# Seven-product passes: a second buffer for the first product's copy, and a hand-laid order on every engine from step 28 on

## The chip, the cores and the metric

The kernel runs on one core of a Trainium2 chip. A core has a matrix engine (PE, TensorE), three engines that work on vectors (DVE, VectorE; ACT, ScalarE; POOL, GpSimd), and queues that move data between HBM and the on-chip memory SBUF; the kernel starts its transfers from SP (SyncE). PE writes into eight accumulator banks of 128x512 numbers. The metric is the device time of one execution, in microseconds (us), smaller is better. The kernel before took 745.49, 742.14 and 744.34 us in three runs, median 744.34.

## The reference

Three stages, each on the result of the one before, all in float32:

```
# 1: attention in chunks of 32 tokens (4 x 8 heads x 768 tokens x 64), with 8 memory keys
a = softmax(0.125 * q_c @ k_full.T);  x = a @ v_full           # x: 3072 x 512
# 2: a feed-forward layer, 512 -> 2048 -> 512
r = maximum(x @ w_in, 0);  y = (s * (r * r) + b) @ w_out        # s, b: one number each
# 3: a soft mixture of 8 experts with 4 slots each
logits = y @ phi                                                # 3072 x 32
slots  = softmax(logits over tokens).T @ y
out    = softmax(logits over slots) @ (maximum(slots @ w1, 0) @ w2)
```

## The kernel before

**Tiles.** The 3072 tokens are six blocks of 512. Every product of stage 2 is worked out from two fp32r pieces: an operand is split into a "high" piece (ACT rounds it) and a "low" piece (DVE or POOL takes the difference), and high x high, high x low and low x high are summed in a bank: three matmuls for one. A split therefore costs an ACT instruction and then a DVE or POOL instruction, and PE waits for the second one.

**Blocks 0 and 1** are worked out in 32 plain steps n. Step n is `mm_h(n)` (12 matmuls, L320, into bank 4 or 5 in turn), `make_g` (L326 to L329: relu on ACT, times on DVE, high on ACT, low on DVE), a few background tasks, and `mm_y(n-1)` (12 matmuls, L339). The background tasks are pieces of attention units u = 0 to 23 (four to a block): `qk` (L192, followed by exp and norm on DVE and ACT), `tr` (a transpose, L221, that ACT L224 and DVE L228 copy out of the bank) and `pv` (L235, copied out by ACT L241, for blocks 2 to 5 as raw x). From step NF-4 on, `pv` uses the bank of L320 that the next step's `mm_h` will use.

**Blocks 2 to 5** are worked out in two calls of `super_block(s)`, each for two blocks and in eight passes p. A pass does a 2x2 block product with seven products instead of eight (`prod`, L623, six matmuls, some 1.36 us each): a11, s1, s2, then 12 matmuls of the second layer (L339) for the pass before, s4, s3, 12 more, a22, a12. All seven go through four banks A, B, C, D. The product a11 stays in bank A: its copy c11 is taken out of it by ACT L687, then s2 is added onto it in the same bank. At the end of the pass, a12 is added to c11 (DVE L722), c11 is squared through a relu (ACT L637, DVE L638) and split into the tile G[0] (ACT L633, DVE L634). c21, from a22, gets the same chain into G[1]. c11 and c21 are the two halves of the tile y0.

`w_sums` (POOL L596) makes the sums of the weights that a pass needs, `w_split` (ACT L615, POOL L616) splits them, `wo_split` (ACT L628, POOL L629) those of the second layer; `wi_load` and `wo_load` bring the weights. In the passes of s = 0 the pieces of units 17 to 23 stand between the products. In the first passes also stand the tasks of the third stage for an older block (`log`, `etr`, `ytr`, `slot`): `log` runs a chain of small DVE instructions and three ACT instructions (L372, L377, L379). After its passes `super_block` has 16 `t2` jobs of 12 matmuls, with the x sums and splits for the next call beside them, or with the loads of the experts' weights.

**Order.** PE and SP run in the order of the program text. ACT, DVE and POOL run in an order that the framework's scheduler chose from its own cost model, except in the opening and the last stage. On every engine the instructions start strictly one after the other: an instruction that waits holds up all behind it.

Of the kernel before, what the change touches and what calls it, by code (L numbers as in the profile page):

```python
# [38 lines left out]
def tile_attention_moe_softmoe(  # L39
# [532 lines left out]
    def wi_load(p):  # L572
        sp.dma_start(out=fresh(f"sp{4 + p}") if p < 2 else cur[f"sp{4 + p % 2}"], in_=DWI[p])
# [57 lines left out]
    def g_split(t, dst):  # L631
        g = hl(dst)
        act.activation(out=r32(g[:, 0]), in_=t, func=AF.Identity, bias=b_col)  # L633
        dve.scalar_tensor_tensor(out=r32(g[:, 1]), in0=t, scalar=b_col, in1=g[:, 0], op0=ALU.add, op1=ALU.subtract)  # L634

    def square(out, h, r):
        act.activation(out=r, in_=h, func=AF.Relu, scale=1.0 / WSCALE ** 2)  # L637
        dve.scalar_tensor_tensor(out=out, in0=h, scalar=s_col, in1=r, op0=ALU.mult, op1=ALU.mult)  # L638

    def super_block(s, pending):  # L640
# [10 lines left out]
        def spot(p, k):  # L651
            if (p, k) in routing:
# [3 lines left out]
            if s == 0:  # L656
                u = 4 * NHP + p
                if k == 1 and p < NPR - 1:
                    run_bg("qk", u + 1, D)
                elif k == 2:  # L660
                    run_bg("pv", u, B)
                elif k == 3 and p < NPR - 1:
                    run_bg("tr", u + 1, D)

        gring = ["sp4", "sp5", "g1", "g0"] * 2 + ["sp5", "g1", "g0"] * 3
        wring = ["sp6", "wi1", "wo1", "wo0"] * 2 + ["rt1", "wo1", "wo0"] * 3
# [15 lines left out]
        fresh("rt1")  # L682
        for p in range(NPR):
            if p + 1 < NPR:
                wi_load(p + 1)
# [6 lines left out]
            if p + 1 < NPR:
                w_sums(p + 1)
                w_split(0, p + 1)
                w_split(1, p + 1)
            else:
                prep(0)
# [7 lines left out]
            square(cur[G2[p]], CH[1], cur["rt1"])  # L705
            if p + 1 < NPR:
# [18 lines left out]
            if p + 1 < NPR:  # L725
                w_split(3, p + 1)
            spot(p, 3)
            pending.append(lambda p=p: mm_job(yp, WO[1], G[1], p == 0, False))
            pending.append(lambda p=p: mm_job(yp, WO[0], G[0], False, p == NPR - 1))
            if s and p == 0:  # L730
                for t in [cur[f"x0{h}"] for h in range(NHP)] + Q + K + V + PB + [EP]:
                    e_free(t)

# [6 lines left out]
        if s == 0:  # L740
# [17 lines left out]
            task(12, w_split, 3, 0)  # L758
        else:
# [6 lines left out]
            for i, t in ((5, "sp4"), (5, "sp6"), (6, "wi1"), (10, "w10"), (10, "w11"), (10, "w12"), (10, "w13"),  # L766
                         (14, "g0"), (14, "wo0"), (15, "sp5"), (15, "wo1"), (15, "g1")):
# [23 lines left out]
    with tc.manual_schedule(engines={mybir.EngineType.PE, mybir.EngineType.SP}):  # L791
# [61 lines left out]
        for n in range(NSTEP):  # L853
# [4 lines left out]
            if n == NSTEP - 1:  # L858
                w_sums(0)
                w_split(0, 0)  # L860
            mm_h(n, (3,) if n == 0 else (0, 1, 2, 3))
# [16 lines left out]
            if n in (NF + 3, NF + 7, NF + 11):  # L878
                for kt in range(2):
                    if n == NF + 11:  # L880
                        x_sum("t1", 0, kt)
                    x_split({3: "b11", 7: "b21", 11: "t1"}[n - NF], 0, kt)
            if n in (NF + 13, NF + 15):
                kt = (n - NF - 13) // 2
                x_sum("t2", 0, kt)
                x_split("t2", 0, kt)
                x_split("b22", 0, kt)
                x_sum("t3", 0, kt)
                x_split("t3", 0, kt)
# [6 lines left out]
            if n == NSTEP - 1:
                w_split(1, 0)
                w_split(2, 0)
                w_split(3, 0)
# [257 lines left out]
```

## Time and profile before

| | |
|---|---|
| runs | 745.49, 742.14, 744.34 us, median 744.34 |
| profiled execution | 743.28 us |
| its span, first to last instruction | 741.5 us |
| busy in the span | PE 678.4, DVE 412.2, ACT 387.0, POOL 289.5 us |
| plain steps 28 to 31 | about 210 to 242 us |
| passes of s = 0, its t2 jobs | about 242 to 417, 417 to 478 us |
| passes of s = 1, its t2 jobs | about 478 to 631, 631 to 685 us |

Busy PE time is made of matmuls at the clock that the chip grants to TensorE: PEclk 1.00 is the upper of its two levels, 0.50 the lower. A stretch is therefore worth two readings, the part of it in which PE stands idle, and the clock in the rest.

### The profile page before, as it was taken

What the parts mean: (1) busy time and instruction counts of PE and PEld (TensorE: products, weight loads), DVE (VectorE), ACT (ScalarE), POOL (GpSimd) and SP (SyncE); (2) the same over time, 40 slices, a digit from 0 to 9 for tenths busy, and PEclk for the clock granted to TensorE, in tenths of its full rate; (3) what the DMA queues carried; (4) which work ended last, traced back from release to release, by engine and by line L of the source; (5) the groups of instructions that cost most, each with busy time, mean ns of one, the idle gap of its engine ahead of it and who ended that gap; (6) DMA issues with size and microseconds to landing.
All of it is one profiled execution on the core that took longest, in us unless ns stands there. A gap on an engine that the chain in (4) does not pass through costs nothing.

```text
span 741.5 us, 12554 instructions
## 1 busy us (share of the span) xinstructions
PE 678.4 (91%) x4983; PEld 528.2 (71%) x4983; DVE 412.2 (56%) x692; ACT 387.0 (52%) x688; POOL 289.5 (39%) x261
## 2 busy tenths in 40 slices
PE   7899999999999788898888799986998888999996
PEld 4678888888788567777766487864776666787474
DVE  4899986665567566544555646445333333532423
ACT  4898864655455455444445555444444544643322
POOL 4100001333458645445555647437355653422000
PEclk9999999999999899999999899999999999999998
DMA  9999945632435132333210230083101110998796
GB/s 333 408 378 371 340 143 197 188 128 92 138 119 194 57 139 93 139 121 108 86 57 28 78 122 29 29 333 149 57 21 40 72 44 23 359 400 301 284 375 270
DMA packets 37786, 126.90 MB, mean 171 GB/s; under 512 B 4192, under 2 KB 4192, under 8 KB 37728
## 3 DMA queue, kind: packets, MB, share of 16 engines
q1 hardware_dynamic: 37728, 126.11, 45.8%
q8 instruction: 39, 0.64, 0.4%
q14 instruction: 19, 0.16, 0.1%
HBM read 111.41 MB, written 14.68 MB: 170 GB/s over the span
## 4 chain that ended last, share of the span: by engine, by line
PE 69%; DVE 8%; DMA 8%; ACT 6%; POOL 6%; issue 2%; SPq 1%; DVEq 0%; POOLq 0%; ACTq 0%
PE bank L339 33%; PE bank L623 12%; PE bank L320 9%; DVE g L634 3%; PE bank L192 3%; PE bank L235 2%; PE bank L1019 2%; ACT g L633 2%; PE bank L978 2%; PE bank L387 2%; DMA sp4n<-dwi 2%; DMA sp<-wd 1%; DVE y L638 1%; POOL sp6n L596 1%; DMA q<-e1d 1%
## 5 line engine op out<-in xcount | busy, mean ns | idle before, releaser
L339 PE MATMUL bank<-g,wo 128*128 128x512 f32 x984 | 247.9, 403 | 0.0
L339 PEld LDWEIGHTS bank<-g,wo 128*128 128x128 f32 x984 | 185.4, 193 | 43.5 <-issue 2.5
L320 PE MATMUL bank<-x,wi 128*128 128x512 f32 x384 | 93.1, 391 | 0.2 <-DVE x L251 0.2
L629 POOL TENSOR_TENSOR wo<-yt,wo 128x512 fp32r<-128x512 f32 x36 | 48.8, 1355 | 92.5 <-ACT wo L628 92.5
L320 PEld LDWEIGHTS bank<-x,wi 128*128 128x128 f32 x384 | 71.8, 188 | 15.5 <-DVE x L251 0.6
L304 POOL TENSOR_TENSOR wi<-w,wi 128x512 fp32r<-128x512 f32 x16 | 20.5, 1281 | 112.6 <-ACT wi L300 111.3
L628 ACT ACTIVATE wo<-yt 128x512 fp32r<-128x512 f32 x36 | 22.7, 630 | 44.1 <-PE bank L339 43.8
L623 PE MATMUL bank<-w6n,wi1n 128*128 128x512 f32 x48 | 16.9, 464 | 31.4 <-ACT y L687 31.2
L702 DVE TENSOR_TENSOR y<-bank,y 128x512 f32<-128x512 f32 x16 | 11.1, 692 | 58.5 <-PE bank L623 58.3
L634 DVE SCALAR_TENSOR_TENSOR g<-y,cons,g 128x512 fp32r<-128x512 f32 x32 | 34.9, 1089 | 12.4 <-ACT g L633 11.5
L327 DVE SCALAR_TENSOR_TENSOR rt<-bank,cons,rt 128x512 f32<-128x512 f32 x32 | 23.9, 746 | 28.7 <-ACT rt L326 28.5
L313 POOL TENSOR_TENSOR wo<-w,wo 128x512 fp32r<-128x512 f32 x16 | 21.1, 1318 | 44.4 <-ACT wo L312 44.4
L623 PEld LDWEIGHTS bank<-w6n,wi1n 128*128 128x128 f32 x48 | 8.7, 205 | 38.3 <-ACT y L687 37.3
L300 ACT ACTIVATE wi<-w 128x512 fp32r<-128x512 f32 x32 | 20.1, 627 | 29.4 <-PE bank L320 29.4
L312 ACT ACTIVATE wo<-w 128x512 fp32r<-128x512 f32 x32 | 20.1, 628 | 23.8 <-PE bank L339 23.0
L192 PEld LDWEIGHTS bank<-k,q 128*64 128x64 f32 x704 | 24.7, 150 | 8.1 <-issue 5.7
L633 ACT ACTIVATE g<-y,cons 128x512 fp32r<-128x512 f32 x32 | 22.9, 715 | 11.4 <-DVE y L638 11.4
L235 PEld LDWEIGHTS bank<-pb,v 128*64 128x64 f32 x704 | 22.4, 138 | 8.9 <-issue 3.8
L192 PE MATMUL bank<-k,q 128*64 128x64 f32 x704 | 27.7, 237 | 1.1 <-ACT ep L208 1.1
L638 DVE SCALAR_TENSOR_TENSOR y<-bank,cons,rt 128x512 f32<-128x512 f32 x16 | 12.0, 750 | 30.1 <-ACT rt L637 29.4
L329 DVE SCALAR_TENSOR_TENSOR g<-rt,cons,g 128x512 fp32r<-128x512 f32 x32 | 25.9, 809 | 3.1 <-ACT g L328 2.6
L616 POOL TENSOR_TENSOR w14n<-sp6n,w14n 128x512 fp32r<-128x512 f32 x16 | 21.3, 1328 | 14.6 <-ACT w14n L615 14.6
(489 smaller groups left out, 1546.2 us busy)
## 6 DMA issues: line engine op xcount, KB each, us to landing
sp<-wd SPq DMA_DIRECT2D x24, 512.0 KB, 9.8
k<-kd SPq DMA_DIRECT2D x22, 512.0 KB, 5.2
v<-vd SPq DMA_DIRECT2D x22, 512.0 KB, 3.6
q<-qd SPq DMA_DIRECT2D x20, 512.0 KB, 3.9
yt<-dwo SPq DMA_DIRECT2D x18, 512.0 KB, 3.3
dwi<-w SPq DMA_DIRECT2D x16, 256.0 KB, 7.2
dwo<-w SPq DMA_DIRECT2D x16, 256.0 KB, 7.2
sp4n<-dwi SPq DMA_DIRECT2D x8, 512.0 KB, 4.2
```

What stands on the lines that cost most here:

```text
L192: pe.matmul(S[64 * par:64 * par + 64, 2 * i + z, :], lhsT=qt[:, c].rearrange("p h n -> p (h n)"), rhs=kt[:, c, :], start=True, stop=True)
L235: pe.matmul(b[64 * h:64 * h + 64, 64 * m:64 * m + 64], lhsT=vt[:, m, h, :], rhs=pb[:, m // 2, m % 2, h].rearrange("p z n -> p (z n)"), sta ...
L320: pe.matmul(HB[n % 2], lhsT=r32(w[:, a, kt, :]), rhs=r32(x[:, b]), start=(kt == 0 and i == 0), stop=(kt == 3 and i == 2))
L327: dve.scalar_tensor_tensor(out=t, in0=HB[n % 2], scalar=s_col, in1=r, op0=ALU.mult, op1=ALU.mult)
L329: dve.scalar_tensor_tensor(out=r32(g[:, 1]), in0=t, scalar=b_col, in1=g[:, 0], op0=ALU.add, op1=ALU.subtract)
L339: pe.matmul(yb[dt], lhsT=r32(w[:, a, dt * 128:dt * 128 + 128]), rhs=r32(g[:, b]), start=(first and i == 0), stop=(last and i == 2))
L616: pool.tensor_tensor(out=r32(lo), in0=src, in1=hi, op=ALU.subtract)
L623: pe.matmul(b, lhsT=r32(wv[:, a, kt, :]), rhs=r32(xv[:, c]), start=(first and kt == 0 and i == 0), stop=(kt == 1 and i == 2), skip_group_c ...
L628: act.activation(out=r32(t[:, 0]), in_=src, func=AF.Copy)
L629: pool.tensor_tensor(out=r32(t[:, 1]), in0=src, in1=t[:, 0], op=ALU.subtract)
L633: act.activation(out=r32(g[:, 0]), in_=t, func=AF.Identity, bias=b_col)
L634: dve.scalar_tensor_tensor(out=r32(g[:, 1]), in0=t, scalar=b_col, in1=g[:, 0], op0=ALU.add, op1=ALU.subtract)
```

## The change

- The copy of a11 goes to the two halves of y0 in turn (`p % 2`). c21 loses its half there and stays, with its relu and square, in one half of the tile rt0; the square of c11 goes into the other half (t11).
- The split of t11 into G[0] moves from the end of a pass behind the c11 copy of the next pass (`finish`). The two copies of a transpose move behind that as well; the transposes themselves stay at the end of the pass.
- `w_sums` and the weight splits of a pass are spread over it in another order; `wi_load(p + 2)` is issued inside pass p, where `wi_load(p + 1)` stood at its head.
- Units 8 to 16 of the attention, and the x splits, come one plain step earlier. The `pv` of unit 15 now stands in step 29 and uses bank 4, that of unit 16 in step 31, bank 4 too, which is bank A of the first pass. `w_sums(0)` moves to step 30.
- From step 28 to the last t2 job ACT, DVE and POOL run in the order of the program text.

```diff
     for u in range(2 * NHP, 4 * NHP + 1):
-        n0 = NF - 3 + 2 * (u - 2 * NHP)
+        n0 = NF - 4 + 2 * (u - 2 * NHP)
...
-        c11, c21 = hl(CH[0])[:, 0], hl(CH[0])[:, 1]
-        r11, r21 = hl(RT[0])[:, 0], hl(RT[0])[:, 1]
+        t21, t11 = hl(RT[0])[:, 0], hl(RT[0])[:, 1]
...
+        def finish(p):
+            g_high(t11, G[0])
+            g_low(t11, G[0])
+
         for p in range(NPR):
-            if p + 1 < NPR:
-                wi_load(p + 1)
+            c11 = hl(CH[0])[:, p % 2]
+            more = p + 1 < NPR
             prod(A, "a11", "b11", p)
             act.activation(out=c11, in_=A, func=AF.Copy)
+            if p:
+                finish(p - 1)
+                if s == 0:
+                    att_place(4 * NHP + p, D)
+            if more:
+                w_sums(p + 1)
+            w_split(3, p)
+            wi_load(p + 2)
             prod(C, "s1", "t1", p)
             act.activation(out=c22, in_=C, func=AF.Copy)
+            if more:
+                w_split(0, p + 1)
+            else:
+                prep(0)
             prod(A, "s2", "t2", p, False)
...
-            square(c21, A, r21)
-            g_split(c21, G[1])
+            prod(A, "a22", "t4", p, False)
+            relu(t21, A)
+            times(t21, A, t21)
+            prod(B, "a12", "b21", p)
             dve.tensor_tensor(out=c11, in0=B, in1=c11, op=ALU.add)
-            square(c11, c11, r11)
-            g_split(c11, G[0])
-            if p + 1 < NPR:
-                w_split(3, p + 1)
-            spot(p, 3)
+            g_high(t21, G[1])
+            relu(t11, c11)
+            g_low(t21, G[1])
+            times(t11, c11, t11)
+            if s == 0 and more:
+                att_turn(4 * NHP + p + 1, D)
...
-            if n in (NF + 13, NF + 15):
-                kt = (n - NF - 13) // 2
+            if n in (NF + 12, NF + 14):
+                kt = (n - NF - 12) // 2
                 x_sum("t2", 0, kt)
-                x_split("t2", 0, kt)
-                x_split("b22", 0, kt)
                 x_sum("t3", 0, kt)
-                x_split("t3", 0, kt)
+                for op in ("b22", "t2", "t3"):
+                    x_split(op, 0, kt)
                 x_sum("t4", 0, kt)
                 x_split("t4", 0, kt)
...
+            if n == NSTEP - 2:
+                w_sums(0)
...
+        for n in range(NSTEP - 4):
+            plain_step(n)
+        with tc.manual_schedule(engines={mybir.EngineType.Activation, mybir.EngineType.DVE, mybir.EngineType.Pool}):
+            for n in range(NSTEP - 4, NSTEP):
+                plain_step(n)
+            super_block(0, [last_plain, lambda: None])
+            super_block(1, [lambda: y_evac(yb=bank[4:8]), lambda: None])
```

On ACT at the turn from one pass of s = 1 to the next, before. y0 holds c11 and c21, rt0 the relus, bank 0 is bank A; L637 is a relu, L633 a high piece, L687 the copy of a11:

```order
L637 ACTIVATE rt0_97<-bank0_159 128x512
L615 ACTIVATE w15n_3976<-sp4n_3882 128x512
L633 ACTIVATE g1_96<-y0_109,cons_66 128x512
L637 ACTIVATE rt0_97<-y0_109 128x512
L633 ACTIVATE sp4n_4801<-x10n_2385,cons_66 128x512
L633 ACTIVATE g0_95<-y0_109,cons_66 128x512
L689 ACTIVATE y1_110<-bank2_161 128x512
L615 ACTIVATE wi0n_3929<-sp5n_4026 128x256
L687 ACTIVATE y0_109<-bank0_159 128x512
```

The same place now (L650 is the relu, L643 the high piece, L702 the copy of a11):

```order
L635 ACTIVATE wo0_85<-yt1_108 128x512
L650 ACTIVATE rt0_97<-bank0_159 128x512
L643 ACTIVATE g1_96<-rt0_97,cons_66 128x512
L650 ACTIVATE rt0_97<-y0_109 128x512
L702 ACTIVATE y0_109<-bank0_159 128x512
L643 ACTIVATE g0_95<-rt0_97,cons_66 128x512
L622 ACTIVATE w15n_4038<-sp4n_3884 128x512
L712 ACTIVATE y1_110<-bank2_161 128x512
```

The copy of a11 stood behind the high piece of g0 and two more; it now stands ahead of it, directly behind the relu of c11.

On ACT in steps 28 to 30, before. bank 5 and bank 4 are those of `mm_h`, L326 the relu and L328 the high piece of `make_g`, L241 the copy of a `pv`, L563 a high piece of an x split:

```order
L208 ACTIVATE ep_111<-ep_111 128x512
L615 ACTIVATE w14n_2379<-sp6n_2319 128x512
L326 ACTIVATE rt0_97<-bank4_163 128x512
L615 ACTIVATE wi0n_2324<-sp4n_2183 128x256
L241 ACTIVATE x03n_1382<-bank5_164 128x512
L328 ACTIVATE g0_95<-rt0_97,cons_66 128x512
L563 ACTIVATE w9n_2365<-x03n_1382 128x512
```

The same copy (unit 15, now L247) and what stands ahead of it now; L569 is the x split's high piece, L306 and L318 the high pieces of `split_wi` and `split_wo`, L332 and L334 the relu and the high piece of step 29:

```order
L208 ACTIVATE ep_111<-ep_111 128x512
L569 ACTIVATE w8n_2220<-x02n_1328 128x512
L569 ACTIVATE w6n_2223<-x00n_1326 128x512
L569 ACTIVATE w10n_2226<-x00n_1326 128x512
L569 ACTIVATE w12n_2230<-x00n_1326 128x512
L306 ACTIVATE wi0_83<-w14_81 128x512
L318 ACTIVATE wo1_86<-w13_80 128x512
L332 ACTIVATE rt1_98<-bank5_164 128x512
L334 ACTIVATE g1_96<-rt1_98,cons_66 128x512
L247 ACTIVATE x03n_1329<-bank4_163 128x512
```

The copy now stands behind four x splits and behind the whole of step 29's chain on ACT, and it reads bank 4, which `mm_h(30)` takes next. On ACT at the head of the first pass, as it is now (L622 is a weight split, L247 the copy of unit 16's `pv`):

```order
L318 ACTIVATE wo1_86<-w15_82 128x512
L622 ACTIVATE wi0n_2349<-sp4n_2233 128x256
L622 ACTIVATE w14n_2352<-sp6n_2342 128x512
L332 ACTIVATE rt1_98<-bank5_164 128x512
L334 ACTIVATE g1_96<-rt1_98,cons_66 128x512
L622 ACTIVATE wi1n_2371<-sp6n_2342 128x512
L247 ACTIVATE x00n_1326<-bank4_163 128x512
L702 ACTIVATE y0_109<-bank4_163 128x512
```

The copy of unit 16 used to stand in the first pass, out of bank B; it now reads bank 4, the bank of the first product, behind two weight splits that wait for `w_sums(0)`.

## Rows read from the trace of the kernel before

**Rows 1.** The page: busy us, share of the span and instructions of each engine.
```profile
PE 678.4 (91%) x4983; PEld 528.2 (71%) x4983; DVE 412.2 (56%) x692; ACT 387.0 (52%) x688; POOL 289.5 (39%) x261
```

**Rows 2.** Waits: engine, line, waited for; us in total, times, longest.
```profile
PE bank L623 <- ACT y L687: 31.2, 13, 3.5
```

**Rows 3.** Stretches: us, busy PE, PEld, DVE, ACT, POOL, clock, DMA, GB/s.
```profile
240.00:265.00 25.00, 21.24 (x162) 15.97 (x161) 14.26 (x24) 13.48 (x27) 14.57 (x13) 0.86 0.20 64
265.00:417.00 152.00, 134.43 (x935) 105.78 (x933) 84.91 (x129) 75.62 (x130) 79.07 (x71) 0.98 0.25 91
417.00:431.00 14.00, 9.57 (x30) 7.30 (x30) 8.70 (x11) 7.95 (x14) 6.38 (x5) 0.76 0.62 235
431.00:478.00 47.00, 47.00 (x246) 37.59 (x246) 25.23 (x35) 23.91 (x45) 26.76 (x22) 1.00 0.09 31
478.00:521.00 43.00, 33.93 (x168) 25.67 (x167) 19.12 (x30) 20.00 (x38) 23.20 (x25) 0.94 0.54 208
521.00:631.00 110.00, 98.12 (x396) 76.41 (x395) 40.40 (x48) 48.80 (x79) 52.99 (x49) 0.93 0.12 43
```

**Rows 4.** Timeline, turn of two passes: start, length, engine, line, [idle before, releaser].
```profile
591.72 0.69 DVE L722 TENSOR_TENSOR y<-bank,y 128x512 f32<-128x512 f32 x1
591.80 0.97 PE L623 MATMUL bank<-w0n,wi0n 128*128 128x512 f32 x3
592.20 1.30 POOL L616 TENSOR_TENSOR w15n<-sp4n,w15n 128x512 fp32r<-128x512 f32 x1 [1.20 <-ACT w15n L615]
592.64 0.62 ACT L637 ACTIVATE rt<-y 128x512 f32<-128x512 f32 x1
592.77 1.27 DVE L634 SCALAR_TENSOR_TENSOR g<-y,cons,g 128x512 fp32r<-128x512 f32 x1 [0.36 <-ACT g L633]
593.97 0.74 DVE L638 SCALAR_TENSOR_TENSOR y<-y,cons,rt 128x512 f32<-128x512 f32 x1
594.74 0.72 ACT L633 ACTIVATE g<-y,cons 128x512 fp32r<-128x512 f32 x1 [0.48 <-DVE y L638]
595.49 0.75 DVE L634 SCALAR_TENSOR_TENSOR g<-y,cons,g 128x512 fp32r<-128x512 f32 x1
596.28 0.60 ACT L687 ACTIVATE y<-bank 128x512 f32<-128x512 f32 x1
596.93 0.96 PE L623 MATMUL bank<-w6n,wi1n 128*128 128x512 f32 x3 [2.11 <-ACT y L687]
```

**Rows 5.** PE alone, passes of s = 1.
```profile
580.64 2.88 PE L339 MATMUL bank<-g,wo 128*128 128x512 f32 x12
...
593.97 0.84 PE L623 MATMUL bank<-w5n,wi1n 128*128 128x512 f32 x3
...
597.73 1.40 PE L623 MATMUL bank<-w7n,wi1n 128*128 128x512 f32 x3
598.93 3.98 PE L339 MATMUL bank<-g,wo 128*128 128x512 f32 x12
```

**Rows 6.** Timeline, end of the first pass of s = 0, with `log`.
```profile
263.73 0.60 ACT L637 ACTIVATE rt<-bank 128x512 f32<-128x512 f32 x1 [0.97 <-PE bank L623]
...
264.56 0.20 ACT L379 ACTIVATION_READ_ACCUMULATOR ets<-bank,nm 128x1 f32 x1
```

**Rows 7.** Chain of waits, second pass of s = 1: start, us, what.
```profile
495.55 11.24 DMA sp4n<-dwi
```

**Rows 8.** PE alone, the first pass of s = 0.
```profile
246.66 1.19 PE L623 MATMUL bank<-w4n,wi1n 128*128 128x512 f32 x2 [2.95 <-ACT g L328]
...
254.26 3.04 PE L339 MATMUL bank<-g,wo 128*128 128x512 f32 x12
...
260.96 1.15 PE L235 MATMUL bank<-pb,v 128*64 128x64 f32 x32
```

**Rows 9.** ACT and DVE in steps 30 and 31.
```profile
234.97 0.59 ACT L241 ACTIVATE x03n<-bank 128x512 f32<-128x512 f32 x1
237.01 1.78 DVE L564 TENSOR_TENSOR w9n<-x03n,w9n 128x512 fp32r<-128x512 f32 x1
```

More of the change, by code (lines that the diff above doesn't have):

```diff
@@ L572, in wi_load @@
     def wi_load(p):
-        sp.dma_start(out=fresh(f"sp{4 + p}") if p < 2 else cur[f"sp{4 + p % 2}"], in_=DWI[p])
+        if p < NPR:
+            sp.dma_start(out=fresh(f"sp{4 + p}") if p < 2 else cur[f"sp{4 + p % 2}"], in_=DWI[p])
     def rw(p):
@@ L631, in g_split, with g_high, g_low, relu @@
     def g_split(t, dst):
+        g_high(t, dst)
+        g_low(t, dst)
+    def g_high(t, dst):
+        act.activation(out=r32(hl(dst)[:, 0]), in_=t, func=AF.Identity, bias=b_col)
+    def g_low(t, dst):
         g = hl(dst)
-        act.activation(out=r32(g[:, 0]), in_=t, func=AF.Identity, bias=b_col)
         dve.scalar_tensor_tensor(out=r32(g[:, 1]), in0=t, scalar=b_col, in1=g[:, 0], op0=ALU.add, op1=ALU.subtract)
-    def square(out, h, r):
+    def relu(r, h):
         act.activation(out=r, in_=h, func=AF.Relu, scale=1.0 / WSCALE ** 2)
+    def times(out, h, r):
         dve.scalar_tensor_tensor(out=out, in0=h, scalar=s_col, in1=r, op0=ALU.mult, op1=ALU.mult)
@@ L651, in spot @@
         def spot(p, k):
+            if s == 0 and k == 2 and p:
+                run_bg("pv", 4 * NHP + p, B)
             if (p, k) in routing:
@@ L655, in spot @@
                 run_bg("csoft", jr)
[L656 to L666, printed above, removed]
+            if s == 0 and k == 1 and p < NPR - 1:
+                run_bg("qk", 4 * NHP + p + 1, D)
+        gring = ["sp4", "sp5", "g1", "g0"] * 2 + ["sp5", "g1", "g0", "sp5"] + ["g1", "g0"] * 2
+        wring = ["sp6", "wi1", "wo1", "wo0"] * 2 + ["rt1", "wo1", "wo0", "rt1"] + ["wo1", "wo0"] * 2
         def prep(i):
@@ L682, in super_block @@
         fresh("rt1")
+        def finish(p):
+            g_high(t11, G[0])
+            g_low(t11, G[0])
         for p in range(NPR):
[L684 to L685 removed]
+            c11 = hl(CH[0])[:, p % 2]
+            more = p + 1 < NPR
             prod(A, "a11", "b11", p)
             act.activation(out=c11, in_=A, func=AF.Copy)
+            if p:
[6 more added lines that the diff above has]
+            wi_load(p + 2)
             prod(C, "s1", "t1", p)
             act.activation(out=c22, in_=C, func=AF.Copy)
+            if more:
+                w_split(0, p + 1)
+            else:
+                prep(0)
             prod(A, "s2", "t2", p, False)
             act.activation(out=c12, in_=A, func=AF.Copy)
[L692 to L694 removed]
+            if more:
                 w_split(1, p + 1)
[L696 to L697 removed]
             spot(p, 1)
@@ L704, in super_block @@
             dve.tensor_tensor(out=c22, in0=A, in1=c22, op=ALU.add)
-            square(cur[G2[p]], CH[1], cur["rt1"])
-            if p + 1 < NPR:
+            relu(cur["rt1"], CH[1])
+            times(cur[G2[p]], CH[1], cur["rt1"])
+            if more:
                 w_split(2, p + 1)
@@ L757, in super_block @@
             task(11, w_split, 2, 0)
-            task(12, w_split, 3, 0)
+            task(11, wi_load, 1)
         else:
@@ L850, in tile_attention_moe_softmoe, with plain_step @@
                 steps[token[0]](int(token[1:]))
-        for n in range(NSTEP):
+        def plain_step(n):
             j, f = divmod(n, NF)
@@ L858, in tile_attention_moe_softmoe @@
             if n == NSTEP - 1:
-                w_sums(0)
                 w_split(0, 0)
+                w_split(2, 0)
             mm_h(n, (3,) if n == 0 else (0, 1, 2, 3))
@@ L893, in tile_attention_moe_softmoe @@
                 wi_load(0)
+                wi_load(1)
                 wo_load(0, YT[0])
                 wo_load(1, YT[1])
[L896 to L899, printed above, removed]
+            if n == NSTEP - 2:
+                w_sums(0)
         def last_plain():
```

33 lines of the change are left out of this document (15 added, 18 removed).

## The prediction

> **What bounds the kernel now.** I read the busy shares first. PE works in 91% of the span [rows 1], so time is saved only where PE stands idle or runs at the lower clock. The table of waits comes next: its largest entry for PE's own instructions is L623 waiting for ACT L687, 31.2 us in 13 waits [rows 2], one for nearly every pass. Third comes the table of stretches, since the change acts on some of them alone. For each I take two numbers: idle = length less PE's busy time, and clock loss = busy time x (1 - PEclk) [rows 3]:
>
> - turn from the plain steps, 240 to 265: 3.8 idle + 3.0 clock = 6.7
> - passes of s = 0, 265 to 417: 17.6 + 2.7 = 20.3
> - start of the t2 jobs, 417 to 431: 4.4 + 2.3 = 6.7
> - the other t2 jobs of s = 0, 431 to 478: nothing
> - first passes of s = 1, 478 to 521: 9.1 + 2.0 = 11.1
> - the other passes of s = 1, 521 to 631: 11.9 + 6.9 = 18.8
>
> Together 63.6 us. The fourth view, the timeline over one turn of passes, shows the wait's cause [rows 4]. a12 is added to c11 at 591.72, relu at 592.64, square at 593.97, high piece at 594.74, and DVE reads c11 once more at 595.49 for the low piece. Only then may ACT overwrite it, at 596.28, with the copy of an a11 whose last matmuls began long before, about 592.6. s2 adds onto the same bank and begins at 596.93, after 2.11 us of idleness. The next rows of PE show what comes on top: three matmuls take 1.40 where they took 0.84, and a job of twelve 3.98 where it took 2.88, the granted clock being lower behind the pause [rows 5].
>
> **1. Second buffer for c11, split of t11 moved behind the copy.** The copy now waits for a11 alone. The relu of c11 stands ahead of it on ACT and ends at 593.26 [rows 4]; a11, at 591.80 plus twice 0.84 less the overlap, ends near 593.2. So the copy would end at some 593.9; s1 takes another 1.36 (four groups of three in the 2.8 us up to the last one's end at 594.81 [rows 5]), so s2 is due at about 594.75. There is 0.8 us of slack, and no wait. The high and low piece of t11 come behind it, 0.72 and 0.75 to 1.27 [rows 4]; the job that needs them is the second of the pass, 6 us later, so they cost nothing. If that cover were gone, the price would be the old wait.
>
> In passes 3 to 7 of s = 1 nothing else changes on the path. I count the whole 18.8 less 0.3 for seams: **-18.5**.
>
> **2. Passes of s = 0.** The same wait goes: 20.3. Two things come back.
>
> The pass with `log`: now ACT runs in the order of the text, and relu(t21) stands behind the chain of `log` and the high piece of WO0. Before it ran at 263.73, ahead of the last of them at 264.56 [rows 6]. The new start is 264.76 and a high piece (0.60, as the relu beside it), 265.4, 1.7 later, and a11 of the next pass needs the square that follows. With the clock behind a pause of that size (0.56 + 1.10 in rows 5, less for a short one) I take 2.9; bounds 0 and 4.
>
> The `qk` tasks write to bank D, which the copies of the transposed unit must have left. They now stand on DVE behind the low piece of t11: square done some 2.9 after a11's start (594.71 - 591.80 [rows 4]), high piece 0.72, low piece 0.75 to 1.27, copy 0.69, together 5.1 to 5.6, against three products of 1.36 and the transpose before them, 4.5 to 4.9. So 0.6 in three passes and 0.2 in two where another task stands ahead, 2.2; bounds 0, and 1.7 in each of six. The row shows why the long value counts: the low piece took 1.27 while POOL ran L616, and 0.75 alone [rows 4]. The Trainium skill ("SBUF — State Buffer", section "Who interferes with whom") says more: a Vector instruction with two SBUF inputs and a GpSimd one that reads SBUF exclude each other, and the loser waits for the whole instruction. The 1.27 beside 0.75 agrees; by that rule alone the added `w_sums` and splits beside the low piece could make the wait up to 2.2 per pass, and this term 13 in place of 2.2.
>
> 20.3 - 2.9 - 2.2: **-15.2**.
>
> **3. Start of the t2 jobs of s = 0.** The idleness here is behind the last pass's squares, and their order by hand puts what the first jobs need first. 6.7 less 0.3: **-6.4**; bounds 0 and -6.7.
>
> **4. The other t2 jobs.** Here PE had no idle time, and POOL and ACT ran in a chosen order. In the text's order the splits for a later job stand behind the `log` chain on ACT and behind the x sums on POOL (1.30 each by L616 [rows 4]). I count one job late by 2.2 and two by 0.7: **+3.7**; bounds 0 and 8.
>
> **5. First passes of s = 1.** The chain there is a weight load of 11.24 us [rows 7], issued behind thirteen loads of expert weights. `wi_load(2)` now is issued in pass 0, ahead of them; `wi_load(3)` stands behind them, and is needed one pass later. Of the 11.1 I give back one `log` pass as in 2, 3.2: **-7.9**; bounds -3 and -11.
>
> **6. Turn from the plain steps (28 to 31) to the first pass.** Before: 2.95 idle at 246.66 for a high piece [rows 8], 6.7 in all. Now two banks are late. Bank 4 for `mm_h(30)` waits for unit 15's copy, which ran without delay before (0.59 at 234.97 [rows 9]). Count from the end of `mm_h(28)`. On PE: transpose 0.5 (an estimate from the 1.15 of `pv`), `qk` like `pv`, three jobs of 2.88 [rows 5] and `pv` 1.15 [rows 8]: due at 11.4. Ahead of the copy: relu, times, high, low (0.60 + 0.75 + 0.72 + 0.75), a copy, reduce and subtract on DVE (3 x 0.69), exp 0.62, norm 1.8 (two of 0.69 and two small ones, an estimate), two low pieces 1.4, an x sum on POOL that waits for the second of them 1.30, three high pieces of 0.60, then relu, times, high 2.1 and the copy 0.59: 14.5, with some 0.04 at each of about 20 hand-overs 15.3 [rows 4, 6, 9]. That is 4 late; where POOL runs beside the low pieces (1.78 [rows 9]) up to 6.2; taken 5.1. In the same way the first a11 waits for unit 16's copy, behind a split that waits for `w_sums(0)`, which stands on POOL behind that second x sum: from the start of `mm_h(30)`, 16.7 against 13.2, 3.5 to 5, taken 4.2. With about 4 of lower clock behind them (before, after 2.95 idle, 3.04 for a job of twelve still [rows 8]) the new turn costs 13.3, against 6.7: **+6.6**; bounds -6.7 and +8.6.
>
> **7. Step 15.** The `pv` of units 7 and 8 now stand together and use one bank: the second waits for the copy and the subtraction of the first, 0.59 + 0.69 and hand-overs: **+1.5**; bounds 0 and 2.7.
>
> The sum: -18.5 - 15.2 - 6.4 + 3.7 - 7.9 + 6.6 + 1.5 = -36.2. From the profiled execution, 743.28 (span 741.5 and 1.8 around it; 1.1 under the runs' median of 744.34), that gives 707.1: **forecast 707 us**.
>
> **The rivals.**
>
> *A. The order by hand is clean:* no new wait in 4 and 6, none in the `log` passes. For it: ACT is busy 52% and DVE 56% of the span [rows 1], so small shifts in their start may let queues run ahead of my walk. Against it: instructions start in order, and the copy of unit 15 is behind an x sum that can't start early. Without 3.7, 6.6 and the 2.9 of the first `log` pass the sum is -49.4, without the second's 3.2 too -52.6: 691 to 694. Chance 0.20.
>
> *B. The wait moves to `qk`:* DVE and POOL hold each other up in all passes of s = 0. Six waits of 1.7, and the lower clock behind each (about 0.8, half of what 2.11 us cost in rows 5), are 15 in place of 2.2: the 15.2 shrinks to 2.4, and the time is 720. For it: 1.27 against 0.75 [rows 4]. Against it: in two or three passes POOL is elsewhere at that moment. Chance 0.17.
>
> *C. The change does not remove the wait:* the copy of a11 stands behind the relu of c11 in ACT's queue, and that waits for DVE's sum. If DVE's sum came 3 later in each pass, s2 would wait as before; of the terms 3 to 7 and the loads' part of 5 (about 5) remain, -6.4 + 3.7 + 6.6 + 1.5 - 5, and the time is about 744. Against it: the sum started before a11 [rows 4], and the relu's start gives 0.8 to spare. Chance 0.05.
>
> *D. Slower: a11 itself waits.* It overwrites bank A, which the square of t21 reads, and in ACT's fixed queue the relu of t21 stands behind the high piece of WO0. The old slack is nil (a11 at 591.80 began right behind the square). Say it starts 3 us later in all 14 passes, as it does by 1.7 in a `log` pass: each pays 3 and 1.6 of clock, 64, against 13 x 3.6 = 47 removed; with -6.4 + 3.7 + 6.6 + 1.5 the time is 765, at 2.3 us 756. It decides from about 1.6 us a pass. Against it: the high piece needs only the second job, and has the whole of a22, 1.36, to run in. Chance 0.05.
>
> **How the numbers follow.** The forecast's own case, each term within its bounds, has 0.53. The range from 690 to 724 takes in most of A and B; under 2 in 10 is left for C, D and a cleaner or dirtier sum. No change can be told from a change within 0.5%, 3.7 us. Faster 0.91 (the forecast, A, B and a little of C), same 0.04 (C), slower 0.05 (D).
>
> **What would show it.** In the passes: no PE wait of L623 for the copy of a11 (now L702); the stretch of the last five passes of s = 1 at 91 to 92 us where it was 110, at clock 1.00. In the turn: `mm_h(30)` waiting 3 to 6 us for L247, a11 of the first pass 3 to 5 us for L247. In the first `log` pass: a11 waiting 1.5 to 3 for the square (L653). In s = 0: `qk` (L192) waiting 0.2 to 1 for L234. It is wrong if s2 still waits over a microsecond, or if the turn shows no wait.

## The result, and the profile after

The changed kernel took 724.44 us (median of four runs, 723.39 to 728.35) against 744.91 for the kernel before on the same chip: ratio 0.9724, 95% interval 0.9652 to 0.9795. It is faster, as forecast, but by 20 us and not by 36; 724.44 lies just above the stated range.

The profiled execution happened to be the longest, 728.35 (span 726.6); its trace is called the new profile below. A second profile of the same kernel, span 721.8, is used for the lengths of stages. First the table of waits, rows of PE, of the new profile (us in total, times, longest):

```profile
PE bank L393 <- DVE ep L207: 5.4, 3, 2.1
PE bank L630 <- DVE rt L653: 5.2, 8, 3.0
PE bank L345 <- POOL wo L636: 4.7, 3, 2.4
PE bank L326 <- ACT x03n L247: 4.0, 1, 4.0
PE bank L630 <- ACT x00n L247: 3.7, 1, 3.7
...
PE bank L345 <- ACT sp5n L643: 2.4, 1, 2.4
PE bank L192 <- DVE pb L234: 2.2, 4, 0.9
```

The 31.2 us of [rows 2] are gone: no entry names the copy of a11, now L702. The largest entry is one that the prediction does not have: L393, a transpose of the third stage, waiting for DVE L207, the subtraction of an attention unit. The turn of two passes, to be compared with [rows 4] (start, length, engine, line, [idle before, releaser]; rows in between are left out):

```profile
585.43 0.69 DVE L742 TENSOR_TENSOR y<-bank,y 128x512 f32<-128x512 f32 x1
585.56 0.96 PE L630 MATMUL bank<-w0n,wi0n 128*128 128x512 f32 x3 [0.18 <-DVE rt L653]
586.21 0.64 ACT L650 ACTIVATE rt<-y 128x512 f32<-128x512 f32 x1
587.25 0.60 ACT L702 ACTIVATE y<-bank 128x512 f32<-128x512 f32 x1 [0.40 <-PE bank L630]
587.49 1.23 DVE L653 SCALAR_TENSOR_TENSOR rt<-y,cons,rt 128x512 f32<-128x512 f32 x1
588.43 0.84 PE L630 MATMUL bank<-w6n,wi1n 128*128 128x512 f32 x3
```

The copy starts at 587.25, 0.40 after ACT was free for it, ends at 587.85, and s2 follows s1 at 588.43 without a pause. The stretches that answer to [rows 3], in the same columns; the first is new:

```profile
146.00:214.00 68.00, 58.58 (x471) 46.55 (x470) 30.62 (x61) 27.71 (x50) 19.25 (x15) 0.92 0.30 101
241.00:272.00 31.00, 23.23 (x144) 18.10 (x143) 13.67 (x22) 14.27 (x26) 17.92 (x16) 0.89 0.31 122
272.00:424.00 152.00, 147.10 (x1052) 118.02 (x1053) 88.70 (x139) 79.99 (x142) 89.52 (x76) 0.98 0.28 98
424.00:490.00 66.00, 57.43 (x277) 44.18 (x276) 44.10 (x51) 30.78 (x58) 45.09 (x33) 0.97 0.20 72
490.00:526.00 36.00, 32.85 (x168) 26.04 (x167) 15.87 (x24) 20.09 (x38) 19.82 (x17) 0.95 0.64 246
526.00:616.00 90.00, 89.12 (x394) 71.18 (x393) 45.57 (x54) 48.72 (x82) 63.44 (x55) 1.00 0.16 54
```

The last one is the stretch that had 11.9 idle and a clock of 0.93; now 0.9 and 1.00. The first one is new as a place of loss: plain steps 18 to 25, 9.4 idle and a clock of 0.92. Before, PE had no wait and the upper clock there:

```profile
145.00:212.00 67.00, 67.00 (x594) 54.48 (x594) 38.55 (x70) 35.11 (x65) 25.73 (x21) 1.00 0.34 117
```

With the second profile the stages compare as follows. Marks are starts of PE's rows: step 12, the first a11, the first t2 job of s = 0, the first product of s = 1, the end.

| stage | before | after | difference |
|---|---|---|---|
| to step 12 | 101.63 | 101.36 | -0.3 |
| step 12 to the first a11 | 140.56 | 167.61 | +27.1 |
| passes of s = 0 | 174.22 | 151.68 | -22.5 |
| t2 jobs of s = 0 | 61.26 | 65.81 | +4.6 |
| s = 1 and the end | 263.83 | 235.34 | -28.5 |

### The profile page after: what moved, and what is told of

Same layout as the page of the kernel before. It is cut to its first block, busy times and chain, and to the rows that moved or that the text cites. A ratio compares the mean times of both kernels' runs of the same rounds, so it can differ in the third digit from the quotient of the medians.

```text
span 726.6 us, 12554 instructions
## 1 busy us (share of the span) xinstructions
PE 673.3 (93%) x4983; PEld 527.3 (73%) x4983; DVE 420.5 (58%) x692; ACT 380.3 (52%) x688; POOL 308.3 (42%) x261
## 4 chain that ended last, share of the span: by engine, by line
PE 69%; DVE 10%; ACT 6%; POOL 6%; issue 5%; DMA 2%; SPq 0%; DVEq 0%; ACTq 0%; POOLq 0%
PE bank L345 30%; PE bank L630 15%; PE bank L326 9%; PE bank L241 3%; PE bank L192 2%; DVE rt L653 2%; PE bank L1043 2%; PE bank L1002 2%; POOL x00n L576 1%; DMA v<-vd 1%; POOL wo L636 1%; PE bank L393 1%; ACT rt L650 1%; POOL x01n L576 1%; POOL sp6n L603 1%
## 5 line engine op out<-in xcount | busy, mean ns | idle before, releaser
L345 PE MATMUL bank<-g,wo 128*128 128x512 f32 x1008 | 254.4, 403 | 6.1 <-POOL wo L636 4.7
L345 PEld LDWEIGHTS bank<-g,wo 128*128 128x128 f32 x1008 | 188.6, 192 | 52.2 <-POOL wo L636 6.0
L326 PE MATMUL bank<-x,wi 128*128 128x512 f32 x384 | 95.8, 399 | 4.3 <-ACT x03n L247 4.0
L326 PEld LDWEIGHTS bank<-x,wi 128*128 128x128 f32 x384 | 73.5, 193 | 20.7 <-ACT x03n L247 4.5
L333 DVE SCALAR_TENSOR_TENSOR rt<-bank,cons,rt 128x512 f32<-128x512 f32 x32 | 23.9, 747 | 56.2 <-ACT rt L332 56.1
L623 POOL TENSOR_TENSOR w14n<-sp6n,w14n 128x512 fp32r<-128x512 f32 x16 | 29.6, 1847 | 37.1 <-ACT w14n L622 37.1
L650 ACT ACTIVATE rt1n<-y 128x1024 f32<-128x1024 f32 x16 | 17.0, 1061 | 43.1 <-DVE y L727 43.1
L647 DVE SCALAR_TENSOR_TENSOR g<-rt,cons,g 128x512 fp32r<-128x512 f32 x32 | 26.2, 819 | 15.7 <-ACT g L643 15.4
L306 ACT ACTIVATE wi<-w 128x512 fp32r<-128x512 f32 x32 | 20.1, 628 | 27.5 <-PE bank L326 27.5
L318 ACT ACTIVATE wo<-w 128x512 fp32r<-128x512 f32 x32 | 20.2, 632 | 27.2 <-PE bank L345 26.5
L643 ACT ACTIVATE g<-rt,cons 128x512 fp32r<-128x512 f32 x32 | 23.2, 726 | 19.8 <-DVE rt L653 19.8
L241 PEld LDWEIGHTS bank<-pb,v 128*64 128x64 f32 x704 | 23.0, 141 | 10.1 <-issue 4.9
L192 PE MATMUL bank<-k,q 128*64 128x64 f32 x704 | 25.6, 227 | 3.9 <-DVE pb L234 2.2
L335 DVE SCALAR_TENSOR_TENSOR g<-rt,cons,g 128x512 fp32r<-128x512 f32 x32 | 25.0, 781 | 6.1 <-ACT g L334 5.5
L653 DVE SCALAR_TENSOR_TENSOR rt<-bank,cons,rt 128x512 f32<-128x512 f32 x16 | 12.0, 750 | 28.2 <-ACT rt L650 28.2
L241 PE MATMUL bank<-pb,v 128*64 128x64 f32 x704 | 26.0, 228 | 1.6 <-DVE x L257 1.4
```

What stands on the lines that cost most here:

```text
L192: pe.matmul(S[64 * par:64 * par + 64, 2 * i + z, :], lhsT=qt[:, c].rearrange("p h n -> p (h n)"), rhs=kt[:, c, :], start=True, stop=True)
L241: pe.matmul(b[64 * h:64 * h + 64, 64 * m:64 * m + 64], lhsT=vt[:, m, h, :], rhs=pb[:, m // 2, m % 2, h].rearrange("p z n -> p (z n)"), sta ...
L326: pe.matmul(HB[n % 2], lhsT=r32(w[:, a, kt, :]), rhs=r32(x[:, b]), start=(kt == 0 and i == 0), stop=(kt == 3 and i == 2))
L333: dve.scalar_tensor_tensor(out=t, in0=HB[n % 2], scalar=s_col, in1=r, op0=ALU.mult, op1=ALU.mult)
L345: pe.matmul(yb[dt], lhsT=r32(w[:, a, dt * 128:dt * 128 + 128]), rhs=r32(g[:, b]), start=(first and i == 0), stop=(last and i == 2))
L623: pool.tensor_tensor(out=r32(lo), in0=src, in1=hi, op=ALU.subtract)
```

## The experiments

Times are medians of four runs each. The kernel before was run beside each group: 744.48, 746.53, 746.21 and 744.93.

**The plain steps.** In the new profile PE's waits in steps 18 to 24 all stand at tasks of the third stage (columns: start, length, what, [idle before, releaser]):

```profile
151.53 1.08 PE L371 MATMUL bank<-yt,cons 128*32 128x128 f32 x32 [0.97 <-DVE pb L234]
153.84 0.65 PE L393 MATMUL bank<-cons,yt 128*128 128x128 f32 x4 [1.23 <-DVE ep L207]
154.25 3.02 PE L345 MATMUL bank<-g,wo 128*128 128x512 f32 x12
...
171.73 0.66 PE L393 MATMUL bank<-cons,yt 128*128 128x128 f32 x4 [2.00 <-DVE ep L207]
172.14 4.58 PE L345 MATMUL bank<-g,wo 128*128 128x512 f32 x12
...
192.33 5.18 PE L345 MATMUL bank<-g,wo 128*128 128x512 f32 x12
```

The background tasks take banks 6 and 7 in turn. Units one step earlier have `tr` and `qk` in even steps, where `log` and `ytr` of block 0 already stood: four tasks, one behind the other, in two banks. The third waits for the first one's copy, the fourth for the second one's subtraction. After the wait of 2.00 us that ends at 171.73 a job of twelve takes 4.58, after that of 2.13 (at 191.56) 5.18, where it takes 3.02 behind the shorter wait of 1.23 (154.25).

The changed kernel unaltered, for comparison:

> The changed kernel, unaltered, beside the others of this group. Both theories: 724 us, 0.965 to 0.980 of the kernel before. It also says whether the profiled 728.35 was a late start (1.4 us more before step 12 than in the profile of before) and not something in the passes: then the new profile's stretches agree within 0.5 us from step 12 on.

Measured 724.2 (ratio 0.9707, 0.9642 to 0.9772). Step 12 starts 1.6 earlier than in the first profile, the first a11 2.9 and the end 4.8: the start is a third of the difference, not the whole, and the stretches do not agree within 0.5.

The third-stage tasks of block 0 one step later, in the odd steps:

```diff
-    for step, task in ((2, "log"), (2, "ytr0"), (4, "etr"), (4, "ytr1"), (6, "ytr2"), (6, "ytr3"), (6, "csoft"), (8, "slot")):
+    for step, task in ((3, "log"), (3, "ytr0"), (5, "etr"), (5, "ytr1"), (7, "ytr2"), (7, "ytr3"), (7, "csoft"), (9, "slot")):
```

> The changed kernel with the third-stage tasks of block 0 (log, ytr, etr, slot) one plain step later, in the odd steps 19 to 25. Theory 1 (the earlier attention units brought transposes and qk into the same even steps as these tasks, four users of two banks one behind the other): the seven waits of these tasks, 9.4 us in all, go, and with them some 5 us of lower clock: 14 us faster than the changed kernel, about 710. Rival (the plain steps are slower because DVE and ACT carry the x splits and the units earlier, whoever shares a step): the waits move but stay, within 3 us of 724.

Measured 708.95 (0.9500, 0.9448 to 0.9552): 15.3 faster. None of the seven waits is left, and the stretch is whole:

```profile
143.00:205.00 62.00, 62.00 (x535) 50.28 (x534) 35.69 (x66) 31.28 (x57) 23.41 (x19) 1.00 0.38 126
```

The same edit in the kernel before puts the tasks where its `tr` and `qk` stand:

> The kernel before with the third-stage tasks of block 0 one plain step later, in the odd steps, where its transposes and qk stand; all else as before. Theory 1 (sharing a step and its two banks is the whole cause): it loses what the change lost there, 12 to 16 us: 756 to 760, with waits at the lines of ytr, etr and slot for the copy of the transpose (DVE L228) and the subtraction (DVE L207). Rival (the order or the x splits of the changed kernel were needed for it): within 3 us of 744.

Measured 755.45 (1.0121, 1.0072 to 1.0169): 9 slower, 5 to 13 by the interval, so at or below the lower end of what was expected. The seven waits came up with nearly the same lengths, 9.5 us in all. From the start of step 18 to that of step 26 the traces have 59.6 us before, 71.4 in this run and 74.0 in the changed kernel: 11.8 and 14.4 more. Most of the difference lies in the two jobs behind the longest waits, 2.98 and 4.52 here:

```profile
173.88 2.98 PE L339 MATMUL bank<-g,wo 128*128 128x512 f32 x12
...
192.14 4.52 PE L339 MATMUL bank<-g,wo 128*128 128x512 f32 x12
```

The stretch has a granted clock of 0.97 where the changed kernel has 0.92. Sharing the step causes the waits, with the x splits and units where they were; what comes on top depends on whether the clock falls.

**The turn.** The two waits, in the second profile:

```profile
250.61 4.32 PE L326 MATMUL bank<-x,wi 128*128 128x512 f32 x12 [4.04 <-ACT x03n L247]
...
268.97 1.65 PE L630 MATMUL bank<-w0n,wi0n 128*128 128x512 f32 x3 [4.10 <-ACT x00n L247]
```

First, steps 28 to 31 outside the hand order, that of the program text:

> The changed kernel with steps 28 to 31 left to the scheduler's order, hand order from the first pass on. Theory (the copies of units 15 and 16 stand behind the splits in ACT's order): the 4.05 before mm_h(30) goes whole, the 3.72 before the first a11 mostly, and the clock loss: 8 to 11 us faster, 713 to 716. Rival (bank 4 is taken by pv just before its next user, so the wait is there in any order): 0 to 3 us faster, with 4.05 still there or moved to bank 5.

Measured 716.09 (0.9600, 0.9546 to 0.9655): 8.1 faster. Neither copy is waited for; one wait of 3.37, a `pv` for its copied operand (DVE L234), came in. So bank 4 alone is not the cause. The next run keeps the hand order and moves only what stood ahead of the copies, from the ends of steps 28 and 30 to the places behind the `pv` of steps 29 and 31 (`t4` with it, its second half into the first pass):

```diff
+            if n in (NF + 13, NF + 15):
+                kt = (n - NF - 13) // 2
+                for op in ("t2", "b22", "t3"):
+                    x_split(op, 0, kt)
...
-                for op in ("b22", "t2", "t3"):
-                    x_split(op, 0, kt)
...
```

> The changed kernel, its order by hand kept, with the x splits of steps 28 and 30 put behind the copies of units 15 and 16 (into steps 29 and 31), and the last x sum and split into the first pass. Theory (what stood ahead of the two copies on ACT is the cause): the 4.05 before mm_h(30) goes, the 3.72 before the first a11 falls below 1, with their clock 8 to 11 us faster, 713 to 716, as with the scheduler's order. Rival (the splits are then late for s2, s4 and s3 of the first pass): waits of 2 to 4 there, 719 to 723.

Measured 718.21 (0.9621, 0.9576 to 0.9666), 6 faster, between the two. `mm_h(30)` waits 0.57 in place of 4.05, as the theory has it: the splits ahead of the copy were the cause there. a11 still waits 3.02 for unit 16's copy, against the theory, and the late splits cost two waits in the first pass (1.18 and 0.77). The trace shows what holds the second copy: ACT stands 4.75 us at a weight split (w14n) ahead of it, for the sums of `w_sums(0)` on POOL.

```profile
260.50 0.63 ACT L622 ACTIVATE w14n<-sp6n 128x512 fp32r<-128x512 f32 x1 [4.75 <-POOL sp6n L603]
```

**The t2 jobs of s = 0.**

> The changed kernel with ACT, DVE and POOL left to the scheduler's order during the t2 jobs of s = 0 alone. Theory (the order of the text puts splits for a later job behind log and the x sums): the six waits there (2.36, 1.20, 1.12, 0.90, 0.52, 2.39, 8.5 in all) go with some 2 us of clock, 10 us faster, about 714; the stretch from the first t2 job to the first product of s = 1 falls from 65.7 to some 55. Rival (POOL has 45 us of work in 66 there, and the tiles' turns were changed, so it is late in any order): at most 3 us faster, 721 or more.

Measured 725.36 (0.9725, 0.9670 to 0.9780), no gain. Five of the six waits went, but before and in the first job new ones came:

```profile
419.12 0.98 PE L630 MATMUL bank<-w12n,w15n 128*128 128x512 f32 x3 [2.46 <-DVE y L729]
421.82 0.96 PE L630 MATMUL bank<-w2n,w15n 128*128 128x512 f32 x3 [1.03 <-ACT x03n L247]
428.47 4.80 PE L345 MATMUL bank<-sp4n,sp6n 128*128 128x512 f32 x10 [4.54 <-DVE rt L653]
```

The scheduler had moved x sums ahead of the last pass's squares, as it did in the kernel before. Only from the fourth job on:

> The changed kernel with the scheduler's order on ACT, DVE and POOL from the fourth t2 job of s = 0 to the last, the first three by hand. Theory (leaving the order to the scheduler cures the body, and the 8 us that it gave back before lay at the seam, where x sums for later jobs went ahead of the last pass's work): the six waits go, nothing at the seam, 7 to 10 us faster, 714 to 717. Rival (the scheduler moves the work ahead again across the seam): a wait of 3 us or more before or in the first t2 jobs, 720 or more.

Measured 724.44 (0.9691, 0.9655 to 0.9728), no gain, though the first job waits only 0.85: the waits came at other tasks later on, the longest 4.71 for `log`'s exponential. Neither theory nor rival foresaw that. With single instructions moved by hand:

> The changed kernel with, in each t2 job of s = 0, the splits for the job after the next put ahead of the third-stage task, the x sums spread over more jobs and two weight splits a job or two later; by hand as before. Theory (single instructions stand in the wrong place of a queue): the waits of 2.33, 1.0, 0.9 and 0.5 go and the 2.4 at the end halves: 4 to 8 us faster, 716 to 720. Rival (the stretch is short of time on the three engines whatever the order, as two other orders gave 724 and 725): the waits come up elsewhere, 722 to 726.

Measured 722.2 (0.9680, 0.9640 to 0.9720), the rival: 2 faster, and the interval holds the changed kernel's 0.9707. The wait of 2.33 became 1.54, the one at the end stayed 2.38, and two came up elsewhere (0.80 and 1.22). From the first t2 job to the first product of s = 1 the four orders take 65.8, 62.5 (with 3.5 of waits ahead of it), 67.1 and 64.0, the kernel before 61.3; without waits and at the upper clock it would be some 55, an estimate from the busy time of 57.43 at 0.97 in the stretch from 424 to 490. The order decides where the loss falls. Why none of them is rid of it is not settled.

**What carried the gain in the passes.** One buffer in the changed kernel, then two in the kernel before:

```diff
-            c11 = hl(CH[0])[:, p % 2]
+            c11 = hl(CH[0])[:, 0]
```

> The changed kernel with c11 copied into the same half in every pass; order, t11 and the deferred split stay. Theory (the second buffer itself carries the gain): the copy must wait for the square of c11, which ended 2.91 us after a11's start; with the copy 0.6 and a11 and s1 at 2.72, s2 is late by 0.8 to 0.9 and pays 0.5 to 0.8 of clock, in 14 passes: 18 to 24 us slower than the changed kernel, 742 to 748. Rival (taking the split of c11 out of the copy's way carried it, the buffer little): up to 8 us slower, 724 to 732.

Measured 730.52 (0.9777, 0.9741 to 0.9814), only 6 slower: the rival. s2 waits 0.28 to 0.91 in ten passes:

```profile
PE bank L630 <- ACT y L702: 4.6, 10, 0.9
```

Now the kernel before, with the second buffer and c21 and both squares in rt0:

```diff
-        c11, c21 = hl(CH[0])[:, 0], hl(CH[0])[:, 1]
...
-        r11, r21 = hl(RT[0])[:, 0], hl(RT[0])[:, 1]
+        t21, t11 = hl(RT[0])[:, 0], hl(RT[0])[:, 1]
...
+            c11 = hl(CH[0])[:, p % 2]
-            square(c21, A, r21)
-            g_split(c21, G[1])
+            square(t21, A, t21)
+            g_split(t21, G[1])
             dve.tensor_tensor(out=c11, in0=B, in1=c11, op=ALU.add)
-            square(c11, c11, r11)
-            g_split(c11, G[0])
+            square(t11, c11, t11)
+            g_split(t11, G[0])
```

> The kernel before with the second buffer alone: c11 in two halves in turn, c21 and the squares in rt0; split of t11 where it was, order of ACT, DVE and POOL left to the scheduler. Theory (the overwritten tile is the cause, order is not): the 31.2 us of waits for the c11 copy go with their clock, some 40 us: 702 to 710. Rival (the scheduler keeps the copy behind the high piece of g0, which waits for the square): s2 still waits 1 to 2 us a pass, 728 to 742.

Measured 698.39 (0.9346, 0.9311 to 0.9381): 26 faster than the changed kernel, with none of its hand order. No wait for L687 is left. And the same with one buffer:

> The kernel before with c21 and the squares moved to rt0 and split from there, but c11 copied into the same half in every pass: the run of 698.4 without its second buffer. Theory (what freed the copy is that the split no longer reads c11; the buffer adds the last bit): the copy waits for the square alone, s2 is late by 0.3 to 0.9, 4 to 8 us more than 698.4, 702 to 707. Rival (in the scheduler's order the second buffer is needed, as the copy stands late on ACT): 720 to 740.

Measured 719.36 (0.9655, 0.9610 to 0.9699): between theory and rival. The wait halves and stays in 13 passes:

```profile
PE bank L623 <- ACT y L687: 16.1, 13, 2.3
```

The turn of two passes there (ACT and DVE):

```profile
557.04 0.74 DVE L638 SCALAR_TENSOR_TENSOR rt<-y,cons,rt 128x512 f32<-128x512 f32 x1
557.81 0.72 ACT L633 ACTIVATE g<-rt,cons 128x512 fp32r<-128x512 f32 x1 [1.48 <-DVE rt L638]
558.44 0.58 ACT L687 ACTIVATE y<-bank 128x512 f32<-128x512 f32 x1
```

The square ends at 557.78 and the copy could start then; it stands behind the high piece on ACT and starts at 558.44. In the hand order it stands ahead of it. With one buffer the waits are 16.1 us here and 4.6 there, and the second buffer is worth 21 us in one order and 6 in the other. That the copy's place behind the high piece makes this difference is read from the two traces; no run moves the copy alone.

**Loads, and the best of both.** Two buffers in the kernel before, with the loads issued a pass earlier:

> The kernel before with the second buffer alone, as in the run of 698.4, and the loads of the input weights issued one pass earlier (two passes ahead, so in s = 1 the third one ahead of the experts' weights). Theory (the chain there was the load that ran 11.2 us): the waits of 1.52 and 1.51 for POOL in the third pass of s = 1 go, 4 to 6 us faster, 692 to 695. Rival (the load that is moved ahead holds up the next one behind the experts' weights): 697 to 700.

Measured 701.02 (0.9393, 0.9339 to 0.9446), no gain, just above the rival's range and not for its reason: the waits of 1.52 and 1.51 went, but the scheduler answered with others, 4.22 in place of 2.95 at the head of the first pass, 2.58 in place of 1.76 at the second a11 of s = 1, and 1.58 in the t2 jobs.

The old plain steps with the new passes:

> The plain steps of the kernel before (units, x splits and weight splits where they were, the scheduler's order) with the passes and t2 jobs of the changed one, ordered by hand, and the t2 jobs arranged as in the run with the splits first. Theory (what the change lost lies in the plain steps and the turn, and the hand order of the passes is good): 724.3 less 15.3, 1.4, some 7 and 4: 694 to 699. Rival (the hand order of the passes loses too, against the scheduler's with two buffers, 698.4): 700 to 706.

Measured 696.33 (0.9327, 0.9278 to 0.9376), the theory. It is level with 698.39 within the two intervals: against the scheduler's order with two buffers the hand order wins in the passes of s = 0 (151.3 against 155.5) and loses in the t2 jobs behind them (64.0 against 60.5); from s = 1 to the end the two are alike (238.2 and 238.5).

One more edit to that run puts the high piece of WO0 behind the relu of a22:

```diff
-            wo_split(cur[WOR[p % 2]], 0, WO[0])
-            wo_load((p + 2) % NPR, cur[WOR[p % 2]])
             prod(A, "a22", "t4", p, False)
             relu(t21, A)
             times(t21, A, t21)
+            wo_split(cur[WOR[p % 2]], 0, WO[0])
+            wo_load((p + 2) % NPR, cur[WOR[p % 2]])
```

> The run with the old plain steps and the new passes (696.3), with the high piece of WO0 put behind the relu of a22 on ACT. Theory (in the two log passes a11 waits because relu stands behind that piece): each of the two waits, 1.14 and 2.97, falls by about 0.6, 1 to 2 us faster, 694 to 695.5. Rival (the chain of log ahead of the relu decides alone): no change within 1 us, waits as they were.

Measured 695.61 (0.9331, 0.9289 to 0.9373), 0.7 less, which can't be told from no change. The two `log` waits fell by 0.52 each, to 0.62 and 2.45, as the theory has it, but the waits of `qk` rose from four of 0.44 to 0.93 to six of 0.65 to 1.11.

## Why the prediction was wrong

*Step 1, the copy of a11: right.* No wait, slack of 0.6 where 0.8 was forecast. The last five passes of s = 1 ran at clock 1.00, in 90 us where 91 to 92 were named. The cause that the prediction gave was the tile overwritten; the runs split it: own tile for the square 25 us, second buffer 21 (6 in the hand order).

*Step 2, passes of s = 0: right.* The stage is 22.5 shorter. 6.7 of that are the old turn and 1.1 the `pv` that moved out; 2.5 of the new turn fall into it, as the first six groups of three behind the late a11 take 6.6 in place of 4.1. That leaves 17.2 for step 2, against 15.2. The `qk` waits are 2.2 us in all (2.8 in the second profile), the value taken. The 13 that the prediction worked out from the Trainium skill ("SBUF — State Buffer", section "Who interferes with whom": the loser waits for the whole of the other's instruction) did not come, but these waits are no test of that rule (rows that bear on it stand in the last section): the low piece took 0.75 in five of the six passes and 0.95 in one, as POOL's sums had ended before it or nearly so. It was the square ahead of it that ran beside them and took 1.23. One pass:

```profile
312.81 1.28 POOL L603 TENSOR_TENSOR sp6n<-sp5n,sp6n 128x256 f32<-128x256 f32 x1
313.41 1.23 DVE L653 SCALAR_TENSOR_TENSOR rt<-y,cons,rt 128x512 f32<-128x512 f32 x1
314.06 1.19 POOL L603 TENSOR_TENSOR sp6n<-sp5n 128x256 f32<-128x256 f32 x1
315.43 0.75 DVE L647 SCALAR_TENSOR_TENSOR g<-rt,cons,g 128x512 fp32r<-128x512 f32 x1 [0.80 <-ACT g L643]
```

So the 2.2 was met with another instruction stretched than the one it was worked out from, which is partly luck. The `log` pass waits 1.14 for the square and, ahead of it, 1.33 for `ets`, which the prediction had not listed.

*Steps 3 and 4, t2 jobs: the failed size.* The start is clean, as step 3 says (no wait from the first job to 447 in the new profile, 4.00 before). The body costs not 3.7 (its own terms, 2.2 and twice 0.7, make 3.6) but 11: 4.6 more in all, -2.7 forecast. Job 5's 2.36 was foreseen as 2.2; the two waits at POOL are 1.2 and not 0.7. Not foreseen were 2.39 for a `wo_split` behind `w_sums` near the end, 0.9, 0.5 and the lower clock behind the waits. The upper bound of 8 was too low as well. Why every order tried loses some 6 to 12 us there stays open.

*Step 5, s = 1: right.* With passes 3 to 7 it gave 28.5, forecast 26.4. The `log` pass costs 2.97.

*Step 6, the turn: right.* 4.05 and 3.72 were measured (4.04 and 4.10 in the second profile), 5.1 and 4.2 forecast, at the two named places. In the second profile the clock behind them adds 1.4 in `mm_h(30)` and 2.5 in the first groups of the pass: 12.0 in all where 13.3 was forecast, so 5.3 over the old turn and not 6.6. This agrees with the stage from step 12 to the first a11: of its 27.1, 15.3 are the shared steps, 1.4 step 15 and 1.1 the moved `pv`, which leaves 9.3, and 2.5 follow behind a11.

*Step 7, step 15: the step that failed.* Its own wait came as written, 1.42. But the prediction took it for the whole price of the units' earlier start. It did not ask which tasks share the other two banks in steps 18 to 24, and so put at nothing what cost 9.4 us of waits and 5 to 6 more behind them at the lower clock: 15.3 by the run that takes it away again.

So -36.2, +15.3 left out, +7.3 in the t2 jobs, -1.3 at the turn, -2.0 in the passes of s = 0 and -2.1 in s = 1 give -19.0, against -19.7 between the two spans. The two that failed are 22.6 together; the other three came out better by 5.4, and without that the time would lie further above the range. Of the rivals none came. B's time, 720, is the nearest, but `qk` is not where the time went.

## What to carry to other kernels

When an edit shifts a task by one step, list for each step everything that then uses the same two buffers; the price stands where the shifted task lands and not at the edit. Before an order is laid by hand, try the change of data alone: here it gave 48 us, and the order and the shifts around it took 26 back. What a second buffer is worth depends on where the instruction that fills it stands in its queue, 21 us in one order and 6 in the other here, so buffer and queue place are to be priced together.

## What the runs showed of the hardware

Where VectorE and GpSimd work side by side on operands in SBUF, as in [rows 4] and in the t2 jobs, both stretch. In the run with the old steps most of GpSimd's subtractions take some 1.74 there, 1.29 alone, and VectorE's take 1.78, 0.68 alone:

```profile
425.64 1.75 POOL L636 TENSOR_TENSOR rt1n<-w15n,rt1n 128x512 fp32r<-128x512 f32 x1
426.15 1.78 DVE L570 TENSOR_TENSOR w8n<-x02n,w8n 128x512 fp32r<-128x512 f32 x1
427.34 1.74 POOL L636 TENSOR_TENSOR wo<-w15n,wo 128x512 fp32r<-128x512 f32 x1
427.85 1.77 DVE L570 TENSOR_TENSOR w7n<-x01n,w7n 128x512 fp32r<-128x512 f32 x1
...
433.77 0.68 DVE L570 TENSOR_TENSOR w9n<-x03n,w9n 128x512 fp32r<-128x512 f32 x1
...
451.15 1.29 POOL L636 TENSOR_TENSOR wo<-y,wo 128x512 fp32r<-128x512 f32 x1 [0.57 <-ACT wo L635]
```

Read by their ends, they take turns: VectorE's end 0.54 behind GpSimd's (427.39 and 427.93, 429.08 and 429.62), and GpSimd's 1.15 behind VectorE's (427.93 and 429.08). A pair takes 1.70, where the two one after the other would take 1.97. The low piece in [rows 4] ends 0.54 behind POOL's too (593.50 and 594.04). So VectorE's stretch follows what is left of GpSimd's instruction when it starts: 1.24 left at 426.15, 1.10 longer; 0.73 left in [rows 4], 0.52 longer. GpSimd's 0.45 comes about in the same way, and is no fixed price. An instruction of VectorE that reads one operand out of a bank was not stretched beside GpSimd (0.75, in the new profile):

```profile
584.21 1.29 POOL L636 TENSOR_TENSOR wo<-yt,wo 128x512 fp32r<-128x512 f32 x1
584.76 0.75 DVE L653 SCALAR_TENSOR_TENSOR rt<-bank,cons,rt 128x512 f32<-128x512 f32 x1 [1.67 <-ACT rt L650]
```

Seven waits of nearly the same lengths, 9.4 and 9.5 us, cost 14.4 in the changed kernel and 11.8 in the kernel before with its tasks moved; 2.3 of the difference are in the two jobs behind the longest waits (9.76 against 7.50), where the granted clock was lower.
